# Four column tiles of one width in the joined slot's second product, and a new table of order

## The chip, the cores and the metric

The kernel runs on one core of a Trainium2 chip. The metric is the time of one execution in device microseconds; a profile of one such execution shows what each engine did. TensorE (PE in the rows, with its weight loads as PEld) multiplies, VectorE (DVE), ScalarE (ACT) and GpSimd (POOL) do the rest, SyncE (SP) issues most transfers.

## The reference

Two layers stand behind each other. The first is a gated linear recurrence over 4 sequences of 5056 rows of 256 channels; the second sends each of the 20224 rows to at most one of eight experts.

```
a_t = exp(8 * sigmoid(r_gate) * log(clip(sigmoid(a_param))))
x_gated = sqrt(max(1 - a_t * a_t, 1e-6)) * sigmoid(i_gate) * x
h = a_t[:, t] * h + x_gated[:, t]          # for each t; y[:, t] = h
...
do_compute = y @ w_skip > 0                # rows without it leave as they are
e_idx = argmax(y @ w_gate)                 # of the rows with it
h = relu(y @ w1[e]);  out = y + gate * (h @ w2[e])   # w1: 256 x 1024, w2: 1024 x 256
```

## The kernel before

The recurrence works on 40 groups of 512 rows. For each, SP loads the two gates and x, TensorE turns them so that channels lie on partitions, ScalarE and VectorE form decay and input, VectorE scans, and TensorE turns the result back. Then scores are taken (`scores`, `tally`), each row gets a place in its expert's region of a buffer in DRAM (`xs`), and GpSimd writes it there (`send`).

The experts work on slots: 256 or 128 rows of one expert, fetched from its region. A slot is turned (`turn`, L806), split into a half-precision value and its remainder (`turn_hi` on ScalarE, `turn_lo` on VectorE), multiplied by w1 (`mm1`, L827), put through relu (`relu` on ScalarE, L837) with its remainder (`rest` on VectorE, L841), multiplied by w2 (`mm2`, L853), weighed and added (`weighed`, L863), and written out (`put`, L869). Each product is a sum of three, since both factors are split. A slot of 128 rows works in two steps `q` of four 128-column pieces of the hidden layer, a slot of 256 rows in four. 48 slots stand in `STREAM` and run while the recurrence still does; behind them come the rests of the eight regions. Five of these are slots of 128 rows, three, of the experts 3, 5 and 7 (`JOINED`), share one slot of 128 rows with 32, 32 and 64 rows (`LAST`). This is the class `Joined`; its tiles end in `j`. Its `mm1` (L913) writes each expert's rows as columns of one tile. Its `mm2` (L928) has the rows as the columns of the weights that TensorE holds, so it uses a part of TensorE's columns for each expert (`tile_position`), 32, 32 and 64 wide.

In program order the last slots are s46, s52, s54, the joined slot, s48, s49 and s50. An `xrs` buffer, one of three, holds a slot's rows from its fetch until its `put` is done.

Nothing sets the order at run time. Every piece of work is a task; `Plan.order` takes the tasks in the order of the table `ORDER` and gives each of 232 tasks that could run on two engines the engine that `ENGINES` names for it. Each engine then runs its own in that order, and semaphores make it wait for what it reads. A loop for further slots stands behind the last one and runs zero times with these inputs.

Of the kernel before, what the change touches and what calls it, by code (L numbers as in the profile page):

```python
# [22 lines left out]
    "PADDAAAAAAAADAAAAAADDAAADAADAAAAAADAAAADAAAAAAAADAAAAAAAAADAAADAAAAAAAPADADAAAADAAADAADAADDAAAAAAPAA"  # L23
    "ADAAAAAAAAAAAAADAAAPPAAAAAAAAAPPAADAADAAAAAAADPPAAADAAAAAPADDADAPAPAAPAAAAAAPAAAPAAAPAPAAPPAAAPPPAAA"
    "AAAAPAPPAPPAPPPPPAAAAAAAPPAPPAAA"
# [196 lines left out]
def kernel(  # L222
# [657 lines left out]
    class Joined(Slot):  # L880
# [39 lines left out]
        def mm2(self, q):  # L920
            if q == 0:
                self.po = ring("po", [P, ST // P, D], f"po{self.name}")
            hh = self.h.pop(q)[1]
# [315 lines left out]
    for b, ks in enumerate(batches):  # L1239
# [5 lines left out]
        for k in ks:  # L1245
            _, e, rows, _ = stream[k]
            last_of[e] = se
            if k >= full_slots and e in JOINED:
# [5 lines left out]
                if len(parts) == len(JOINED):  # L1254
                    n = joined.nq
# [71 lines left out]
```

## Time and profile before

| | |
|---|---|
| three timed runs | 662.18, 664.52, 665.43 us; median 664.52 |
| the profiled execution | 662.41 us; span from first to last instruction 660.3 us |
| busy in the span | TensorE 577.6, VectorE 509.5, ScalarE 445.7, GpSimd 331.0 us |
| granted TensorE clock, mean | 0.951 |
| the joined slot's second product (L928) | 72 matmuls, 626.62 to 637.33 us |

The busy times are sums over stages with different limits, so a share of the span says little by itself. The granted clock is the share of full speed that TensorE was allowed: 1.00 is 2.4 GHz, 0.50 is 1.2 GHz. A matmul's duration in a row is its way through the array; the next one starts long before it ends, so the step from start to start is read from a row of many.

### The profile page before, as it was taken

The page shows a single profiled execution, that of the slowest core. Times are in us where ns is not written, and L with a number is a line of the kernel's source. Part 1 is how long each engine was busy: PE and PEld are TensorE (multiplying, and loading weights), DVE is VectorE, ACT ScalarE, POOL GpSimd, SP SyncE. Part 2 cuts the span into 40 slices and gives each one's busy share as a digit, 9 for nine tenths or more (in the row PEclk, how much of TensorE's full clock was granted, in tenths as well). Part 3 has the DMA queues.
Part 4 walks back from the last instruction along what each step waited for, and adds up shares of the span by engine and source line. Part 5 has one row for each costly group of instructions (what it writes and reads, how often), then busy time and mean ns, then how long its engine had stood idle before and what let it go on. Part 6 is the DMA issues. An engine that isn't in the chain of part 4 may idle for free. (4 is left out here: it accounts for less than half of the span.)

```text
span 660.3 us, 18625 instructions
## 1 busy us (share of the span) xinstructions
PE 577.6 (87%) x7204; PEld 495.3 (75%) x7204; DVE 509.5 (77%) x1149; ACT 445.7 (68%) x647; POOL 331.0 (50%) x523
## 2 busy tenths in 40 slices
PE   1544489789899999999999999998899999999996
PEld 1333378668787888888788888897798898889865
DVE  2998989879999888898898889798785566443522
ACT  7998887878998886898888886854744423222211
POOL 5456556555574565556564575646466222441201
PEclk9955579999999999999999999999999999999999
DMA  8999988896898687777586653745353312143110
GB/s 307 358 317 337 315 272 277 275 317 188 310 330 257 244 302 247 221 246 231 196 279 221 219 198 103 260 141 174 101 170 137 89 34 89 43 139 116 39 31 22
DMA packets 72408, 134.58 MB, mean 204 GB/s; under 512 B 10291, under 2 KB 42997, under 8 KB 72320
## 3 DMA queue, kind: packets, MB, share of 16 engines
q1 hardware_dynamic: 60560, 112.58, 51.7%
q0 software_dynamic: 11488, 20.82, 8.8%
q8 instruction: 57, 0.93, 0.6%
q14 instruction: 31, 0.25, 0.1%
q10 hardware_dynamic: 272, 0.00, 0.0%
HBM read 89.48 MB, written 54.44 MB: 218 GB/s over the span
## 5 line engine op out<-in xcount | busy, mean ns | idle before, releaser
L827 PE MATMUL phs<-xhs,wsb 128*128 128x128 f16 (+1 forms) x2544 | 231.0, 246 | 7.5 <-DVE hps L841 5.0
L853 PE MATMUL pos<-wsb,hps 128*128 128x256 f16 x1896 | 227.9, 273 | 2.0 <-DVE ots L863 1.0
L709 POOL DMA_INDIRECT xs<-yr,di x158 | 177.7, 1125 | 99.8 <-issue 64.2
L827 PEld LDWEIGHTS <-wsb 128*128 128x128 f16 x2544 | 195.2, 98 | 27.5 <-issue 9.9
L853 PEld LDWEIGHTS <-hps 128*128 128x128 f16 x1896 | 181.5, 98 | 25.6 <-DVE hps L841 2.1
L837 ACT ACTIVATE hps<-phs 128x512 f16<-128x512 f32 x158 | 93.3, 594 | 107.9 <-PE phs L827 92.0
L869 POOL DMA_INDIRECT out_dram<-ots,xrs x79 | 84.1, 1065 | 150.9 <-DVE ots L863 101.3
L841 DVE SCALAR_TENSOR_TENSOR hps<-phs,hps 128x512 f16<-128x512 f32 x158 | 108.1, 687 | 52.6 <-ACT hps L837 52.2
L480 DVE TENSOR_TENSOR_SCAN a<-a,a,m 128x512 f32<-128x512 f32 (+1 forms) x78 | 97.6, 1262 | 0.3
L443 ACT ACTIVATE a<-pt,cc 128x512 f32<-128x512 f32 (+1 forms) x80 | 58.5, 774 | 6.8 <-PE pt L422 6.7
L474 DVE SCALAR_TENSOR_TENSOR m<-m,pt 128x512 f32<-128x512 f32 (+1 forms) x80 | 51.6, 670 | 1.4 <-PE pt L422 1.2
L469 DVE SCALAR_TENSOR_TENSOR i<-i,x 128x1024 f32<-128x1024 f32 (+1 forms) x40 | 48.8, 1220 | 2.3 <-DMA x<-in_x_dram 2.3
L813 ACT ACTIVATE xhs<-pxs 128x256 f16<-128x256 f32 (+1 forms) x53 | 25.9, 489 | 36.3 <-PE pxs L806 29.3
L776 DVE SCALAR_TENSOR_TENSOR wsb<-w,wsb 128x512 f16<-128x512 f32 x64 | 44.0, 699 | 7.6 <-POOL wsb L772 5.7
L863 DVE SCALAR_TENSOR_TENSOR ots<-pos,xrs 128x256 f32<-128x256 f32 x79 | 36.9, 477 | 16.7 <-PE pos L853 16.1
L422 PE MATMUL pt<-ident,r 64*128 64x64 f32 x632 | 31.2, 252 | 19.3 <-ACT r L413 12.8
L502 ACT COPY yr<-py 128x512 f32<-128x512 f32 (+1 forms) x62 | 35.1, 580 | 17.9 <-DVE yr L504 6.4
L422 PEld LDWEIGHTS pt<-ident,r 64*128 64x128 f32 x632 | 26.4, 161 | 24.5 <-issue 11.5
L466 ACT ACTIVATE m<-m,quarter 128x1024 f32<-128x1024 f32 (+1 forms) x40 | 43.4, 1131 | 0.2
L816 DVE SCALAR_TENSOR_TENSOR xhs<-pxs,xhs 128x256 f16<-128x256 f32 (+1 forms) x53 | 29.3, 553 | 18.2 <-ACT xhs L813 18.0
L772 POOL TENSOR_SCALAR wsb<-w 128x512 f16<-128x512 f32 x24 | 24.1, 1006 | 38.1 <-DMA w<-in_moe_w_dram 37.5
L413 ACT ACTIVATE r<-r 128x1024 f32<-128x1024 f32 (+1 forms) x40 | 41.6, 1043 | 1.9 <-DMA r<-in_r_gate_dram 1.8
(130 smaller groups left out, 626.6 us busy)
## 6 DMA issues: line engine op xcount, KB each, us to landing
r<-in_r_gate_dram SPq DMA_DIRECT2D x39, 512.0 KB, 5.6
x<-in_x_dram SPq DMA_DIRECT2D x39, 512.0 KB, 5.9
i<-in_i_gate_dram SPq DMA_DIRECT2D x39, 512.0 KB, 5.1
out_dram<-yr SPq DMA_DIRECT2D x39, 512.0 KB, 4.8
w<-in_moe_w_dram SPq DMA_DIRECT2D x64, 256.0 KB, 4.8
xrs<-xs SPq DMA_DIRECT2D x26, 258.0 KB, 3.5
xrs<-xs SPq DMA_DIRECT2D x27, 129.0 KB, 4.0
xs<-yr,di POOLq DMA_INDIRECT x158
```

What stands on the lines that cost most here:

```text
L422: nc.tensor.transpose(to(pt[:, h]), t[r], ident[r, r], tile_position=(HP * h, 0))
L443: nc.scalar.activation(in_two(ta[g][:, k, :tiles_of(g) * P]), tp[g][:, :, k], AF.Exp, scale=c, bias=c)
L469: nc.vector.scalar_tensor_tensor(ti[g], ti[g], 1.0, tx.pop(g), op0=ALU.add, op1=ALU.mult)
L474: nc.vector.scalar_tensor_tensor(m, m, 0.5e-3, tp[g][:, :, k], op0=ALU.max, op1=ALU.mult)
L480: nc.vector.tensor_tensor_scan(a, a, tm[g][:, k, :n], prev, op0=ALU.mult, op1=ALU.add)
L709: i = nc.gpsimd.indirect_dma_start(out=xs[:, :], out_offset=bass.IndirectOffsetOnAxis(ap=vs[s]["di"][:, c:c + 1], axis=0), in_=yrow[g][:, ...
L776: nc.vector.scalar_tensor_tensor(lo, raw[e, q], SC, hi, op0=ALU.mult, op1=ALU.subtract)
L827: nc.tensor.matmul(ph[:, c, :], lhsT=self.w.w1(k, part, q * self.fp + c), rhs=self.xx[:, xx, k, :], start=(n == 0), stop=(n == 3 * KD - 1),)
L837: nc.scalar.activation(hh[:, 0], self.h[q][0], AF.Relu)
L841: nc.vector.scalar_tensor_tensor(hh[:, 1], ph, 0.0, hh[:, 0], op0=ALU.max, op1=ALU.subtract)
L853: nc.tensor.matmul(self.po[:self.np, j, :], lhsT=hh[:, h, c, j * P:j * P + self.np], rhs=self.w.w2(f, part), start=(f == 0 and j == 0 and ...
L869: i = nc.gpsimd.indirect_dma_start(out=out[:, :], out_offset=bass.IndirectOffsetOnAxis(ap=self.at[:, j, :], axis=0), in_=self.ot.pop(j)[:s ...
```

## The change

It has two parts. The first is in the `mm2` of the joined slot: each expert's rows are cut into tiles of 32, so that 64 rows become two tiles, and all four tiles have one width. Three matmuls for each factor pair become four. The second is the table: `ORDER` and `ENGINES` are other strings (of the table's 109 changed lines one is shown).

```
-0 6 9 10 16 1606 8 1600 1552 7 1612 17 1607 1601 1 2 1608 3 19 20 12 11 1516 1609 1553 13 1613 1610 1602 22 21 23 14
...
+0 6 9 10 1600 16 1606 1573 8 18 7 4 1601 1 2 1574 1607 3 1602 1575 1608 19 11 12 13 20 21 22 23 14 26 15 27 1603 17
...
-                    for o, rows, w in self.parts:
+                    for o, w in [(o + n, w) for o, rows, w in self.parts for n in range(0, rows, 32)]:
                         nc.tensor.matmul(
-                            self.po[o:o + rows, 0, :], lhsT=hh[:, h, c, o:o + rows],
+                            self.po[o:o + 32, 0, :], lhsT=hh[:, h, c, o:o + 32],
                             rhs=w.w2(f, part), start=(f == 0 and part == 0 and h == 0),
                             stop=(f == NF - 1 and h == 1), tile_position=(0, o),
                             skip_group_check=True,
```

Each engine has nearly the same tasks as before. By `ENGINES`, three squares (L453 on ScalarE, L457 on GpSimd), one piece of the weights (L770, L772) and two roundings of y (L565, L567) go from GpSimd to ScalarE, and two copies out of PSUM from VectorE to ScalarE. The filler memsets on GpSimd (L704) are 198 in place of 188. How many tasks stand ahead of a slot, counted in the two orders (before, now):

| | TensorE, ahead of `mm1` | VectorE, ahead of `turn_lo` | ScalarE, ahead of the first `relu` |
|---|---|---|---|
| slot s0 | 35, 36 | 123, 122 | 85, 88 |
| slot s12 | 138, 139 | 328, 316 | 213, 220 |
| slot s24 | 288, 290 | 588, 582 | 367, 376 |
| slot s36 | 431, 431 | 821, 818 | 499, 505 |

On TensorE, in the middle of the joined slot's second product, this stood before (`hpj` are the two tiles of the joined hidden layer, one for each half, `poj` is the result):

```order
L928 LDWEIGHTS hpj_11384
L928 MATMUL poj<-wsb,hpj_11384 32x256
L928 LDWEIGHTS hpj_11384
L928 MATMUL poj<-wsb,hpj_11384 32x256
L928 LDWEIGHTS hpj_11384
L928 MATMUL poj<-wsb,hpj_11384 64x256
L928 LDWEIGHTS hpj_11409
L928 MATMUL poj<-wsb,hpj_11409 32x256
```

That is the last group of the first half, 32, 32 and 64 columns wide, and the first load and matmul of the second half (`hpj_11409`). At the same place now:

```order
L928 LDWEIGHTS hpj_11394
L928 MATMUL poj<-wsb,hpj_11394 32x256
L928 LDWEIGHTS hpj_11394
L928 MATMUL poj<-wsb,hpj_11394 32x256
L928 LDWEIGHTS hpj_11394
L928 MATMUL poj<-wsb,hpj_11394 32x256
L928 LDWEIGHTS hpj_11394
L928 MATMUL poj<-wsb,hpj_11394 32x256
L827 LDWEIGHTS wsb
L827 MATMUL phs_0_11471<-xhs_11466,wsb 128x128
```

A group has four matmuls of 32 columns in place of two of 32 and one of 64; and behind the first half stands the first half of the first product of slot s48 (`phs_0`), where the second half of the joined product stood.

On VectorE, around the joined slot, before (`xhs` is the rounding of the slot behind it, `hps` its hidden layer, `otj` the joined result, weighed; `ots_0_11394` the result of s54):

```order
L1002 CAST tab<-ptab 1x174
L841 SCALAR_TENSOR_TENSOR hpj_11384<-phj_11238,hpj_11384 128x512
L863 SCALAR_TENSOR_TENSOR ots_0_11394<-pos_11201,xrs_10883 128x256
L841 SCALAR_TENSOR_TENSOR hpj_11409<-phj_11311,hpj_11409 128x512
L816 SCALAR_TENSOR_TENSOR xhs_11407<-pxs_11399,xhs_11407 128x256
L863 SCALAR_TENSOR_TENSOR otj_11486<-poj,xrj 128x256
L841 SCALAR_TENSOR_TENSOR hps_0_11538<-phs_0_11488,hps_0_11538 128x512
L841 SCALAR_TENSOR_TENSOR hps_1_11541<-phs_1_11513,hps_1_11541 128x512
```

There the joined result waits for nothing but its product, with the two remainders of s48 behind it. The same stretch of VectorE now:

```order
L1002 CAST tab<-ptab 1x174
L863 SCALAR_TENSOR_TENSOR ots_0_11403<-pos_11208,xrs_10930 128x256
L841 SCALAR_TENSOR_TENSOR hpj_11394<-phj_11248,hpj_11394 128x512
L816 SCALAR_TENSOR_TENSOR xhs_11466<-pxs_11414,xhs_11466 128x256
L841 SCALAR_TENSOR_TENSOR hpj_11468<-phj_11321,hpj_11468 128x512
L841 SCALAR_TENSOR_TENSOR hps_0_11496<-phs_0_11471,hps_0_11496 128x512
L863 SCALAR_TENSOR_TENSOR otj_11548<-poj,xrj 128x256
L841 SCALAR_TENSOR_TENSOR hps_1_11575<-phs_1_11550,hps_1_11575 128x512
L816 SCALAR_TENSOR_TENSOR xhs_11594<-pxs_11591,xhs_11594 128x256
```

The result of s54 is weighed ahead of the joined slot's first remainder and no longer behind it, the rounding of s48 ahead of the second, and the joined result is weighed between the two remainders of s48 and no longer ahead of both.

## Rows read from the trace of the kernel before

**Rows 1.** The page: busy us, share and instructions; TensorE's tenths in 40 slices.

```profile
PE 577.6 (87%) x7204; PEld 495.3 (75%) x7204; DVE 509.5 (77%) x1149; ACT 445.7 (68%) x647; POOL 331.0 (50%) x523
...
PE   1544489789899999999999999998899999999996
```

**Rows 2.** Stages: stretch, length, busy time of each engine, TensorE clock, DMA share, GB/s.

```profile
core 0: us, PE busy (x) PEld busy (x) DVE busy (x) ACT busy (x) POOL busy (x), PEclk, DMA share, GB/s
0.00:33.00 33.00, 10.58 (x136) 7.61 (x137) 21.39 (x40) 26.68 (x31) 15.57 (x29) 1.00 0.92 333
33.00:91.00 58.00, 29.82 (x364) 21.86 (x366) 54.01 (x114) 51.77 (x71) 35.39 (x35) 0.50 0.95 321
91.00:150.00 59.00, 50.85 (x732) 43.04 (x725) 50.86 (x117) 47.27 (x72) 32.88 (x48) 0.97 0.85 277
150.00:626.60 476.60, 459.02 (x5698) 402.69 (x5695) 375.38 (x866) 314.86 (x466) 241.89 (x404) 1.00 0.56 184
626.60:637.30 10.70, 10.70 (x74) 4.91 (x74) 1.02 (x2) 0.87 (x2) 1.16 (x3) 1.00 0.09 25
637.30:660.30 23.00, 16.57 (x221) 15.23 (x220) 6.84 (x12) 4.24 (x8) 4.14 (x6) 0.94 0.08 27
```

**Rows 3.** The end in time: start, us, engine, line, what, count [idle before, releaser].

```profile
626.62 10.71 PE L928 MATMUL poj<-wsb,hpj 128*32 128x256 f16 x72
...
637.26 2.85 PE L827 MATMUL phs<-xhs,wsb 128*128 128x128 f16 x48
637.37 0.48 DVE L863 SCALAR_TENSOR_TENSOR otj<-poj,xrj 128x256 f32<-128x256 f32 x1 [8.71 <-PE poj L928]
...
651.03 2.84 PE L853 MATMUL pos<-wsb,hps 128*128 128x256 f16 x24
...
653.91 0.48 DVE L863 SCALAR_TENSOR_TENSOR ots<-pos,xrs 128x256 f32<-128x256 f32 x1 [1.36 <-PE pos L853]
654.67 0.98 POOL L869 DMA_INDIRECT out_dram<-ots,xrs  x1 [3.04 <-DVE ots L863]
```

**Rows 4.** Line L928: duration ns min/median/max, first and last start, forms.

```profile
L928 PEld LDWEIGHTS <-hpj x72: 91/93/107, 626.6 to 637.0; 128*32 128x32 f16 x48, 128*64 128x64 f16 x24
L928 PE MATMUL poj<-wsb,hpj x72: 282/283/298, 626.6 to 637.0; 128*32 128x256 f16 x48, 128*64 128x256 f16 x24
```

**Rows 5.** TensorE in time, first 0.1 us of L928, then first 0.2.

```profile
626.62 0.29 PE L928 MATMUL poj<-wsb,hpj 128*32 128x256 f16 x2
...
626.62 0.51 PE L928 MATMUL poj<-wsb,hpj 128*32 128x256 f16 x3
```

**Rows 6.** In time, full width: a slot of 256 rows, second product.

```profile
606.20 4.09 PE L853 MATMUL pos<-wsb,hps 128*128 128x256 f16 x36
```

**Rows 7.** Scores, four tiles of 32 columns: in time from 214.4, then L533's durations.

```profile
214.47 0.59 PEld L533 LDWEIGHTS lg<-a,wr 128*32 128x32 f32 x16
214.48 1.07 PE L533 MATMUL lg<-a,wr 128*32 128x256 f32 x16
...
L533 PE MATMUL lg<-a,wr x208: 376/380/636, 27.3 to 311.3; 128*32 128x256 f32 x104
```

**Rows 8.** In time: ScalarE and VectorE on the joined second half.

```profile
627.01 0.59 ACT L837 ACTIVATE hpj<-phj 128x512 f16<-128x512 f32 x1
...
627.63 0.69 DVE L841 SCALAR_TENSOR_TENSOR hpj<-phj,hpj 128x512 f16<-128x512 f32 x1 [1.34 <-ACT hpj L837]
```

**Rows 9.** SP in time: the last fetch; the page: its size, us to landing.

```profile
641.09 0.33 SPq L792 DMA_DIRECT2D xrs<-xs  x1
...
xrs<-xs SPq DMA_DIRECT2D x27, 129.0 KB, 4.0
```

**Rows 10.** ScalarE by form: count | busy us, mean ns | idle before.

```profile
L453 ACT ACTIVATE m<-a 128x1024 f32<-128x1024 f32 x34 | 35.9, 1063 | 1.9 <-DVE a L480 1.7
...
L770 ACT ACTIVATE wsb<-w 128x512 f16<-128x512 f32 x40 | 24.9, 630 | 8.1 <-DMA w<-in_moe_w_dram 7.9
```

More of the change, by code (lines that the diff above doesn't have):

```diff
@@ L22 @@
 ENGINES = (
-    "PADDAAAAAAAADAAAAAADDAAADAADAAAAAADAAAADAAAAAAAADAAAAAAAAADAAADAAAAAAAPADADAAAADAAADAADAADDAAAAAAPAA"
-    "ADAAAAAAAAAAAAADAAAPPAAAAAAAAAPPAADAADAAAAAAADPPAAADAAAAAPADDADAPAPAAPAAAAAAPAAAPAAAPAPAAPPAAAPPPAAA"
-    "AAAAPAPPAPPAPPPPPAAAAAAAPPAPPAAA"
+    "PAAAAADAAAAAADAAAAAAAAAADAAAAAAAAAAAAAAAAAAAAAAADAAAAAAAAADAAADAAADADAPAADDAAAAAAAAAAADDAADAAAAAAPAA"
+    "ADAAADAAPAAADAAADAAAAAAAAADAADPAAAAAADADAAAAADAADDDAAAAADAAAAAAPPAAAAPAAAAAAAAAPAAPAPAPAAPPAAAAPPAAA"
+    "AAAPPPPPAPPAPPPPPAPAAAAAAPAAAAAA"
 )
 ORDER = """
[109 rows of a table removed]
[109 rows of a table added]
 """
```

216 rows, old and new, of the table ORDER are left out of this document.

## The prediction

> **What bounds the kernel now.** I read the page first, then the busy time of each engine by stage, then the end in order of time. On the page TensorE is busy 577.6 us of 660.3, VectorE 509.5, ScalarE 445.7 [rows 1]; the tenths show TensorE idle for the first sixth and at nine or more after it. The stages tell why [rows 2]. From 33 to 91 us VectorE has 54.0 us of work in 58.0 and ScalarE 51.8, while TensorE has 29.8, at a granted clock of 0.50, which is the 1.2 GHz level; it had been busy 10.6 us of the 33 before. So here the recurrence sets the pace. From 150 to 626.6 us TensorE is busy 459.0 of 476.6 us at clock 1.00: that stage is TensorE's, with 17.6 us of gaps. Then comes a stretch that belongs to one line: 10.7 us with 74 matmuls, in which VectorE has 1.0 us of work, ScalarE 0.9 and the DMA engines are at 0.09.
>
> The end in order of time shows that stretch from inside [rows 3]. The second product of the joined slot (L928) runs from 626.62 for 10.71 us. VectorE idles 8.71 us until it ends, and TensorE's next work, the first product of the slot behind it, starts at 637.26. From there three slots of 128 rows follow without a pause (16.57 us busy up to the last row of matmuls, which ends at 653.87), then 0.48 us of VectorE, the last write at 654.67 and some 5 us until the span ends. Nothing else runs beside L928, so each microsecond off it comes off the end, if the three slots behind it stay as dense.
>
> **The edit of the product.** The 72 matmuls have two widths [rows 4]: 48 of 32 columns and 24 of 64, in the order 32, 32, 64. The narrow pair runs side by side: two matmuls of 283 ns each take 0.29 us together [rows 5]. With the third the row is 0.51 us long, and the third lasts 297 ns, so it starts 0.21 us after the pair, and the next pair 0.446 us after the first (10.71 / 24). Two changes of width per triple thus cost 0.21 and 0.23 us. For comparison, a matmul of the full 128 columns with the same 256 moving columns starts every (4.09 - 0.27) / 35 = 0.109 us [rows 6]. A change of width therefore costs some 0.11 us above the streaming.
>
> The change puts four tiles of 32 columns in a row, 96 matmuls in 24 groups of four, with no change of width inside. What four tiles do is in this trace already: the scores of the recurrence (L533) are 16 passes in four groups of four tiles of 32 columns. A pass lasts 0.38 us in the median, and all 16 take 1.07 us [rows 7], so a group follows the one before after about (1.07 - 0.38) / 3 = 0.23 us; that is in fp32, with the same 256 columns; were the four not side by side, 16 passes would need four times that. All 16 weight loads are through 0.59 us after the first begins, while matmuls of earlier groups still run. So I take 0.109 us a group: 24 x 0.109 = 2.62 us. The bounds: not below 2.62, since each group must stream its 256 columns; above, 24 x 0.223 = 5.35 us (half of 0.446) if every group emptied the array as every change of width does now, and 96 x 0.109 = 10.5 us if the four ran one after another, which the pair of rows 5 excludes for two tiles. The value is the one nearest to the scores' row.
>
> The Trainium skill, "TensorE: Matmul & The Clock Gate", section "Part 3: Packing small matmuls — row/col tiling", says that a weight load overlaps running matmuls only where the two use different row groups. All four tiles here use all 128 rows; by that rule each group would show its load. The scores' loads [rows 7] also use all rows and do overlap, so the trace speaks against the rule for this case; what it would give stands below as a rival.
>
> The new order also splits the product. Before, its two halves of 5.3 us stand back to back; now the first half of the next slot's first product (24 matmuls, 2.85 / 2 = 1.43 us) stands between them. That adds two changes of width, 2 x 0.11 = 0.22 us. It is also needed: the second half reads a tile that ScalarE begins at 627.01 and VectorE finishes at 627.63 + 0.69 = 628.32 [rows 8], and the first half would now end at about 626.62 + 1.31 = 627.93. With 1.43 us of other work in between nothing waits; without it 0.4 us would be late. The product then costs 2.62 + 0.22 = 2.84 us: 10.71 - 2.84 = 7.9 us go.
>
> What is late next: the three slots' own steps. ScalarE's and VectorE's steps on a slot's tile (0.60 + 0.69 us and the gaps) were done beside L928 for the first of them; now they have 1.43 us of matmuls beside them, as those of the last slot have already. I allow 0.3 us for small waits, between 0 and 1. The fetch of the last slot waits for the joined slot's buffer: it was issued at 641.09 [rows 9], 3.8 us after L928's end, and such a fetch lands in a median of 4.0 us. In the new order TensorE has 1.43 + 1.31 + 0.22 + 1.31 + 2.85 + 1.31 = 8.4 us of other work between the product and that slot's transposes, against 7.8 us: no wait, but with little to spare; a late landing costs at most a microsecond or two, and this is in the range. Sum here: 7.9 - 0.3 = 7.6 us.
>
> **The edit of the order.** The same 2745 pieces stand in another order, and some change engine. Three squares (1.06 us each on ScalarE), one weight piece (0.63) and two roundings of y go from GpSimd to ScalarE, and two copies from VectorE to ScalarE. The last four are no larger than a weight piece, so at its time ScalarE gains at most 3 x 1.06 + 5 x 0.63 = 6.3 us [rows 10]. From 150 to 626.6 us ScalarE is idle for a third (314.9 us busy of 476.6), and the three squares stand in the program's last third; this hides them. GpSimd's ten more filler memsets hide likewise: it is busy 241.9 us of that stage. The table of counts in the section on the change shows how near the orders are: ahead of slot 0's, 12's, 24's and 36's first product TensorE has the same pieces within two, VectorE 1 to 12 fewer ahead of the slot's rounding, ScalarE 3 to 9 more ahead of its first relu. What this does to the gaps is not in any row: at best it takes half of TensorE's 59.0 - 50.9 = 8.1 us of idle time between 91 and 150 us, 4 us; at worst the moved 6.3 us are paid in full. I take zero, since the nearest row, that of the long stage, shows TensorE 96% busy and so little to win or lose.
>
> Sum against the profiled execution: it took 662.4 us, with a span of 660.3. 662.4 - 7.6 = 654.8. The median of the three timed runs is 664.5, 2.1 above that execution; the same step from it gives 656.9. I predict 656.
>
> **Rivals.** (a) Loads not hidden: each group adds the time of its load to the streaming. A load of 32 columns is a row here, 0.092 us [rows 4], so the product takes 24 x (0.109 + 0.092) + 0.22 = 5.0 us, near the 5.35 of emptied groups. The gain is 10.71 - 5.0 - 0.3 = 5.4, the time 657 to 659. It is the Trainium skill's rule quoted above that would have it so. For it: no row of this trace has four fp16 tiles. Against it: rows 7. 0.11.
>
> (b) The moved work of ScalarE is paid in full: in the startup, where it is busy 51.8 of 58 us, each of its microseconds in front of the first slots' steps delays TensorE. The time is 664.5 - 7.6 + 6.3 = 663.2, no change. For it: rows 2. Against it: the squares that move stand late, where ScalarE has room. 0.17.
>
> (c) The order itself is better: VectorE has less in front of the first slots, and half of TensorE's idle time between 91 and 150 us goes. 656.9 - 4 = 653. 0.16.
>
> (d) Slower: TensorE's clock. It is granted 0.50 from 33 to 91 us and 1.00 behind that [rows 2]; a startup in another order may see it rise later. In the stage behind, TensorE is busy 50.9 us of 59, so a microsecond more at half speed costs up to 0.86 us of doubled work, less the 0.14 us of idle time that can take it up: about 0.7 us. From 11 us later on the gain of the product is gone; at 20 us later it costs 14 us and the time is 664.5 - 7.6 + 14 = 671. For it: the clock stands at the lower level once more, in the mean of 0.97 there. Against it: in both orders the same transfers and products stand in front. 0.06.
>
> **How the numbers follow.** My forecast has 0.50, and with (a) 0.11, (c) 0.16 and the small rest of (b) that ends below 661.2 the chance of faster by over 0.5% is 0.78. Less than 0.5% (3.3 us) is about what a measurement of this kernel can't tell from no change: 0.16, nearly all of it (b). Slower 0.06 is (d). The range reaches from 651 (c, with 2 us for the runs' spread) to 661.5, which takes in (a), the bound of 5.35 us and half of (b).
>
> **What would show it.** In the new profile L928 should show 96 matmuls of one form, in two rows of about 1.5 us with L827 between them, and VectorE's wait for it should fall from 8.71 us to under 3. From the start of L928 to the end of the span there should be about 26 us in place of 33.7. If L928's rows are 2.5 us or longer each, it is (a). If L928 is short and the span did not follow, the first start of L928 tells: it stands at 626.6 now, and (b), (c) and (d) move it. I am wrong if it starts more than 4 us off, or if the slots behind show waits that add up to more than 1 us.

## The result, and the profile after

The changed kernel takes 643.14 us, the median of four runs, where the kernel before takes 664.97: 21.8 us less between the medians. The ratio is 0.9688, 95% interval 0.9645 to 0.9731; by it, 20.7 us went. The forecast was 656, with 651 as the low end of its range. The direction was right and more than half of the gain was missing from the sum. The execution that was profiled took 642.77 us, with a span of 640.9; that of before 662.41, with 660.3. So the two traces differ by 19.4 us of span.

A line of the page of after, for [rows 1]: busy time of the engines.

```profile
PE 566.7 (88%) x7228; PEld 494.0 (77%) x7228; DVE 501.4 (78%) x1147; ACT 450.8 (70%) x655; POOL 332.4 (52%) x527
```

The stages of after, for [rows 2], with the same columns; the last two stretches are the product and what is behind it.

```profile
0.00:33.00 33.00, 11.80 (x154) 9.00 (x156) 20.82 (x44) 28.15 (x32) 15.29 (x29) 1.00 0.92 333
33.00:91.00 58.00, 30.71 (x386) 22.42 (x383) 52.72 (x111) 53.32 (x76) 37.56 (x35) 0.74 0.99 334
91.00:150.00 59.00, 52.47 (x764) 45.84 (x762) 52.76 (x132) 50.03 (x78) 32.91 (x52) 0.97 0.82 272
150.00:614.90 464.90, 452.20 (x5624) 399.22 (x5620) 367.02 (x850) 314.10 (x463) 242.50 (x405) 1.00 0.57 188
614.90:619.30 4.40, 4.40 (x123) 3.80 (x123) 1.81 (x3) 1.47 (x3) 0.00 (x0) 1.00 0.13 34
619.30:640.90 21.60, 15.17 (x196) 13.75 (x195) 6.24 (x11) 3.75 (x7) 4.13 (x6) 0.95 0.09 29
```

The end of after in time, for [rows 3] (start, us, engine, line, what, count, idle before and what ended it), and the forms of the product, for [rows 4].

```profile
614.91 1.49 PE L928 MATMUL poj<-wsb,hpj 128*32 128x256 f16 x48
616.34 1.51 PE L827 MATMUL phs<-xhs,wsb 128*128 128x128 f16 x24
617.78 1.49 PE L928 MATMUL poj<-wsb,hpj 128*32 128x256 f16 x48
619.33 0.48 DVE L863 SCALAR_TENSOR_TENSOR otj<-poj,xrj 128x256 f32<-128x256 f32 x1
...
634.51 0.48 DVE L863 SCALAR_TENSOR_TENSOR ots<-pos,xrs 128x256 f32<-128x256 f32 x1 [1.36 <-PE pos L853]
...
L928 PEld LDWEIGHTS <-hpj x96: 92/97/97, 614.9 to 618.9; 128*32 128x32 f16 x96
L928 PE MATMUL poj<-wsb,hpj x96: 272/273/283, 614.9 to 619.0; 128*32 128x256 f16 x96
```

Read it in two parts, cut at the start of L928. Behind the cut all is as predicted: each half of the product takes 1.43 us (614.91 to 616.34, 617.78 to 619.21), 2.86 in all; VectorE's wait for it is gone; from the start of L928 to the end of the span there are 640.9 - 614.9 = 26.0 us. Ahead of the cut 11.7 us are missing that no term of the sum held: L928 starts at 614.91, and it started at 626.62.

TensorE issues the same 6912 matmuls ahead of L928 in both kernels. Up to the cut it is busy 550.3 us of 626.6 before and 547.2 of 614.9 after, so 8.6 of the 11.7 us are idle time that went, and 3.1 are busy time. Most of the idle time did not go where I had looked: ahead of 91 us it falls by 2.1 us (from 50.6 to 48.5), and between 91 and 150 us it is 59.0 - 52.5 = 6.5 us, where it was 8.1. In the stage behind it falls from 17.6 to 12.7 us, and one stretch loses as much as that, between two points, the starts of the first product of slot s32 (its second quarter) and of slot s39. The first line is before, the second after, by stretch:

```profile
440.10:520.10 80.00, 74.24 (x874) 65.14 (x872) 57.50 (x127) 43.70 (x69) 44.66 (x70) 1.00 0.44 143
```

```profile
434.70:508.60 73.90, 73.40 (x875) 65.89 (x872) 55.41 (x133) 43.31 (x67) 43.77 (x73) 1.00 0.49 158
```

The same 875 matmuls stand with 5.8 us of gaps before and 0.5 after. I call this stretch the late one. Below, "idle in the late stretch" is always this difference, length less TensorE's busy time, between the same two matmuls of a run's own trace.

### The profile page after: what moved, and what is told of

Read it like the earlier page. It is cut to its first block, busy times and chain, and to the rows that moved or that the text cites. A ratio compares the mean times of both kernels' runs of the same rounds, so it can differ in the third digit from the quotient of the medians.

```text
span 640.9 us, 18655 instructions
## 1 busy us (share of the span) xinstructions
PE 566.7 (88%) x7228; PEld 494.0 (77%) x7228; DVE 501.4 (78%) x1147; ACT 450.8 (70%) x655; POOL 332.4 (52%) x527
## 5 line engine op out<-in xcount | busy, mean ns | idle before, releaser
L709 POOL DMA_INDIRECT xs<-yr,di x158 | 186.5, 1180 | 99.2 <-issue 56.8
L827 PE MATMUL phs<-xhs,wsb 128*128 128x128 f16 (+1 forms) x2544 | 231.5, 247 | 3.2 <-DVE hps L841 1.4
L827 PEld LDWEIGHTS <-wsb 128*128 128x128 f16 x2544 | 196.3, 99 | 21.9 <-issue 3.6
L837 ACT ACTIVATE hps<-phs 128x512 f16<-128x512 f32 x158 | 93.7, 596 | 107.2 <-PE phs L827 89.0
L869 POOL DMA_INDIRECT out_dram<-ots,xrs x79 | 86.6, 1097 | 153.3 <-DVE ots L863 87.3
L841 DVE SCALAR_TENSOR_TENSOR hps<-phs,hps 128x512 f16<-128x512 f32 x158 | 107.8, 685 | 56.6 <-ACT hps L837 55.9
L466 ACT ACTIVATE m<-m,quarter 128x1024 f32<-128x1024 f32 (+1 forms) x40 | 43.4, 1131 | 0.2
L413 ACT ACTIVATE i<-i 128x1024 f32<-128x1024 f32 (+1 forms) x40 | 41.8, 1044 | 1.4 <-DMA i<-in_i_gate_dram 1.3
L453 ACT ACTIVATE m<-a 128x1024 f32<-128x1024 f32 (+1 forms) x38 | 39.4, 1046 | 2.4 <-DVE a L480 1.4
```

The costliest lines, as they stand in the source:

```text
L413: nc.scalar.activation(t, t, AF.Tanh, scale=0.5)
L709: i = nc.gpsimd.indirect_dma_start(out=xs[:, :], out_offset=bass.IndirectOffsetOnAxis(ap=vs[s]["di"][:, c:c + 1], axis=0), in_=yrow[g][:, ...
L827: nc.tensor.matmul(ph[:, c, :], lhsT=self.w.w1(k, part, q * self.fp + c), rhs=self.xx[:, xx, k, :], start=(n == 0), stop=(n == 3 * KD - 1),)
L837: nc.scalar.activation(hh[:, 0], self.h[q][0], AF.Relu)
L841: nc.vector.scalar_tensor_tensor(hh[:, 1], ph, 0.0, hh[:, 0], op0=ALU.max, op1=ALU.subtract)
L869: i = nc.gpsimd.indirect_dma_start(out=out[:, :], out_offset=bass.IndirectOffsetOnAxis(ap=self.at[:, j, :], axis=0), in_=self.ot.pop(j)[:s ...
```

## The experiments

Each ratio is to runs of before on the same chip. The runs with the three letters alone, with all letters, with the widths and with the filler were made on a chip on which all takes longer (681.8 us for before). A part "of after's table" means order and engine letters together. The two tables hold the same tasks up to a cut but for one, at 888 and at 1606, so that one can be continued with the other there.

**Product and table apart.** First the new product in the old table:

```
-                    for o, rows, w in self.parts:
+                    for o, w in [(o + n, w) for o, rows, w in self.parts for n in range(0, rows, 32)]:
-                            self.po[o:o + rows, 0, :], lhsT=hh[:, h, c, o:o + rows],
+                            self.po[o:o + 32, 0, :], lhsT=hh[:, h, c, o:o + 32],
```

> The tables of before with the new product alone. Theory (product and order add, as the two traces read: L928 start to span end 33.7 against 26.0 us): 7.7 us under before, ratio 0.988, 657 us where before is 665. Rival (the product needs the new order around it, since its second half would wait for hpj in the old one): at most 4 us under before, ratio 0.994.

655.86 us, ratio 0.9868 (0.9819 to 0.9918), 8.8 us by it: the theory. Here the halves stand back to back, and L928 is one row of 3.03 us with 96 matmuls. The second half's input is late, as predicted, but by no more than that: its first weight load waits 0.33 us for VectorE's L841, where the prediction had 0.4.

Then the new table with the old product:

```
-ENGINES, ORDER = before's
+ENGINES, ORDER = after's
```

> The tables of after with the old product of 72 matmuls in tiles of 32, 32 and 64 columns. Theory: the order alone is worth what L928's start shows, 11.7 us in the profiled executions, to 14 us (the rest of the 21.8 us between the medians): ratio 0.979 to 0.983, 651 to 653 us where before is 665; L928 itself is back at some 10.7 us. Rival (the order gains only because of the four-column product, or the 11.7 us are one execution's chance): ratio over 0.993.

654.24 us, ratio 0.9824 (0.9784 to 0.9863), 11.7 us. The product of the two ratios is 0.9694, and after has 0.9688: the parts add. I had valued the second at zero.

**Where the table gains.** Its halves, cut at task 1606 (slot s23):

```
+ORDER = after[:1606] + [t for t in before if t not in after[:1606]]
```

> Old product. The table of after for its first 1606 tasks (up to slot s23's second product, 336 us), then the remaining tasks in before's order with before's engines; the two tables hold the same tasks up to there but for one. Theory (each stretch is worth what the two traces show for it by itself): L853 of s23 comes 6.4 us earlier and the end with it, ratio 0.990. Rival A (the whole gain is TensorE's clock in the startup, 61.4 against 34.1 us at half speed): ratio 0.980 as the whole table. Rival B (a gain made early is lost again in the late stretch, whose other engines wait for something else): within 0.4% of before.

660.01 us, ratio 0.9918 (0.9877 to 0.9958).

```
+ORDER = before[:1606] + [t for t in after if t not in before[:1606]]
```

> Old product. The table of before for its first 1606 tasks, then the remaining tasks in after's order with after's engines. Theory (stretches add): the waits of TensorE between 440 and 520 us go (5.8 against 0.5 us idle), 5.3 us under before, ratio 0.992. Rival A (all of the gain is made in the startup): within 0.3% of before, with the waits at 440 to 520 us still there. Rival B (the late stretch is the whole gain, the early one only moves it): ratio 0.982.

659.0 us, ratio 0.9907 (0.9876 to 0.9937), and the late stretch shows 0.25 us of idle time:

```profile
440.40:514.00 73.60, 73.35 (x874) 65.89 (x872) 55.48 (x133) 43.28 (x67) 43.86 (x73) 1.00 0.48 159
```

The halves give 0.9826 together, the whole table 0.9824. Both rivals of each fall: neither half is the whole, and no gain is lost later.

The early half was cut once more, to its first 397 tasks (94 us):

```
+ORDER = after[:397] + [t for t in before if t not in after[:397]]
```

> Before, old product; the first 397 tasks (up to slot s1's first product, 94 us) in after's order with after's engines, the rest in before's. Theory (each stretch for itself): TensorE's idle time ahead of s0's first product falls by 2 us (50.4 against 48.3 us in the two first traces), and 2 of the 5.4 us of the early half are there: ratio 0.997. Rival A (the startup is all of the early half): 0.992. Rival B (a gain in the startup is used up by slot s14, since VectorE, 87 us busy of the next 97, is behind anyway): 1.000 with idle at s14 as before's 65.0 us.

661.64 us, ratio 0.9946 (0.9916 to 0.9976), idle ahead of s0's first product 48.4 us: the gain of the startup is clear of zero, but its size is not settled. The interval reaches from 1.6 to 5.6 us and holds both the theory (2 us, 0.997) and rival A (the whole early half, 0.992).

Then to the tasks 888 to 1606:

```
+ORDER = before[:888] + [t for t in after[:1606] if t not in before[:888]] + [the rest, as in before]
```

> Before, old product; only the tasks 888 to 1606 (slot s11's first product to s23's second, 191 to 336 us) in after's order with after's engines. Theory: 3 of the early half's 5.4 us are here, ratio 0.995, idle between s11 and s23 down from 5.8 to under 3 us. Rival (these waits are only the late end of what the startup left behind, VectorE's queue of work): ratio 1.000 and idle 5 us or more.

665.4 us, ratio 0.9976 (0.994 to 1.0011): idle from s11 to s23 4.8 us in place of 5.8, and no change of time that can be told from none; the interval also holds the theory's 0.995. The tasks between 397 and 888 were not tried by themselves.

Two of VectorE's waits in the startup differ plainly. Up to s0's first product, before and then the run with after's first 397 tasks (waited for, us, times, longest):

```profile
DVE wsb L776 <- POOL wsb L772: 5.7, 3, 2.8
```

```profile
DVE i L469 <- ACT i L413: 3.9, 2, 3.3
...
DVE wsb L776 <- ACT wsb L770: 1.7, 2, 1.5
...
DVE wsb L776 <- POOL wsb L772: 1.5, 3, 0.5
```

VectorE waits 2.5 us less for the first parts of weights, but 3.9 us for a gate from ScalarE, a wait that before's list does not have; its idle time up to there is 16.8 us (86.9 less 70.1 busy) and was 15.4 (87.5 less 72.1). So the shorter wait for weights does not explain the startup's gain, and its cause stays open.

**What the late stretch lost.** In before's trace, in time:

```profile
452.59 3.75 POOL L457 TENSOR_TENSOR m<-a 128x1024 f32<-128x1024 f32 x2
452.81 3.63 DVE L619 TENSOR_TENSOR d<-ls 128x64 f32<-128x64 f32 x1
...
456.60 0.68 DVE L841 SCALAR_TENSOR_TENSOR hps<-phs,hps 128x512 f16<-128x512 f32 x1
457.34 0.93 PE L827 MATMUL phs<-xhs,wsb 128*128 128x256 f16 x7 [2.38 <-DVE hps L841]
```

```profile
L619 DVE TENSOR_TENSOR d<-ls x7: 208/216/3628, 339.8 to 554.2; 128x64 f32<-128x64 f32 x6, 128x48 f32<-128x48 f32 x1
```

L619 adds 64 numbers a row, and its seven runs take 0.216 us in the median (the last line: ns, least, median, most). Here it takes 3.63 and ends 0.1 us after GpSimd's two squares of 1024. L841 stands behind it in VectorE's queue, though ScalarE had its input ready at 452.97, and TensorE waits for that. The Trainium skill, "SBUF — State Buffer", section "Who interferes with whom", says that a VectorE instruction with two SBUF inputs contends with a GpSimd instruction that reads SBUF, and that the second to start is blocked until the first is through. The trace agrees that it is held, with 3.63 against 0.216 us; but L619 starts 0.2 us behind the first square and is held through the second as well, which the sentence does not cover. It is no chance of one execution: in the seven traces with the three squares on GpSimd, one instruction of VectorE lasts 3.4 to 4.2 us beside the two that stand together, and in the nine without them none is held for longer than 1.3 us.

The new table puts the squares of groups 36, 37 and 38 on ScalarE. These three letters alone, in the old table with the old product:

```
-    "ADAAAAAAAAAAAAADAAAPPAAAAAAAAAPPAADAADAAAAAAADPPAAADAAAAAPADDADAPAPAAPAAAAAAPAAAPAAAPAPAAPPAAAPPPAAA"
+    "ADAAAAAAAAAAAAADAAAPPAAAAAAAAAPPAADAADAAAAAAADAAAAADAAAAAAADDADAPAPAAPAAAAAAPAAAPAAAPAPAAPPAAAPPPAAA"
```

> Before, with the squares (L457) of the groups 36, 37 and 38 on ScalarE in place of GpSimd: three letters of the string of engines, no other task moved. In before's trace VectorE's L619 of 0.22 us takes 3.63 us at 452.8 beside two of them, and TensorE waits for VectorE's L841 behind it. Theory (this collision is the late stretch's loss): L619 back at 0.22 us, TensorE's idle time between the starts of s32's and s39's first products 5.8 us down to under 1.5 us, ratio 0.992 as for the late half of the table. Rival A (the collision explains the one wait of 2.4 us and the order the rest): idle 3 to 4 us, ratio 0.996. Rival B (ScalarE, with three more tasks, is late instead): ratio 1.000 or over, TensorE waiting for ScalarE there.

Ratio 0.9895 (0.9859 to 0.993), and no instruction of VectorE is held there any more. With before's table on this chip it is another one than L619 (from the widths' run below, whose late stretch is before's), a step of one element a row with a median of 0.15 us:

```profile
466.77 3.80 DVE L951 SCALAR_TENSOR_TENSOR sel<-nxt,base 128x1 f32<-128x1 f32 x1
```

The idle time did not fall to the 1.5 us that the theory had: the late stretch keeps 5.3 us, where the widths' run has 8.7. Part of it is a wait of 2.5 us behind a block of ScalarE's work, which is read below in the run that adds the product. The ratio says 7 us, the trace 3.4.

All 54 letters in the old order:

```
-ENGINES = before's
+ENGINES = after's
```

> Before's order with all 54 changed engine letters of after, old product. Theory: the late stretch's gain is in the letters (5 us) and the early one's in the order, so ratio 0.992, idle at s23 within 1 us of before's 68.4 us. Rival A (letters are all of it): 0.982. Rival B (letters picked for another order collide anew in this one): ratio over 0.998, with new long instructions on VectorE beside GpSimd's.

Ratio 1.0686 (1.0618 to 1.0754): 47 us slower. The sign is rival B's, but neither its size nor its mechanism was expected: no instruction of VectorE is stretched anew. VectorE waits for GpSimd's parts of the weights instead, 25.1 us in six waits, the longest 12.5, where the widths' run has 5.7 us in three:

```profile
DVE wsb L776 <- POOL wsb L772: 25.1, 6, 12.5
```

In the longest of them GpSimd waits for no other engine: it works through eight sends (L709, some 0.98 us each) from 117.7 to 130.2 us, and the weight part, which stands behind them in its queue, starts at 130.27. So the 54 letters as a whole fit only the order they were chosen with. Where the rest of the 47 us goes was not followed.

The reverse, after with the three squares back on GpSimd:

```
-    "ADAAADAAPAAADAAADAAAAAAAAADAADPAAAAAADADAAAAADAADDDAAAADAAAAAAPPAAAAPAAAAAAAAAPAAPAPAPAAPPAAAAPPAAA"
+    "ADAAADAAPAAADAAADAAAAAAAAADAADPAAAAAADADAAAAADPPDDDAAAADPAAAAAPPAAAAPAAAAAAAAAPAAPAPAPAAPPAAAAPPAAA"
```

> After with the squares of groups 36, 37 and 38 back on GpSimd, three letters. Theory (the collision with VectorE is in the letters and not in before's order): a VectorE instruction of two inputs from SBUF is held up by some 2 to 3.5 us beside L457, and TensorE's late stretch (s32 to s39) idles 2 to 4 us more than after's 0.5 us: ratio to before 0.973 to 0.976. Rival (the new order has slack there or puts no such instruction beside them): 0.969 as after.

652.67 us, ratio 0.98 (0.9752 to 0.9848), somewhat more than expected, and 5.8 us of idle time are back in the late stretch. Another instruction of VectorE is held up beside the squares, L658. It reads one tile, and its row begins 0.36 us ahead of the first square's, so it has neither two inputs nor is it the second to start. In time, with a stretch in the columns of [rows 2] as the last line:

```profile
454.59 4.15 DVE L658 TENSOR_SCALAR sg<-sg 128x8 f32<-128x8 f32 x1
...
454.95 3.75 POOL L457 TENSOR_TENSOR m<-a 128x1024 f32<-128x1024 f32 x2
455.90 1.48 PE L827 MATMUL phs<-xhs,wsb 128*128 128x256 f16 x12
458.74 2.19 ACT L466 ACTIVATE m<-m,quarter 128x1024 f32<-128x1024 f32 x2 [4.34 <-POOL m L457]
461.31 1.06 ACT L502 COPY yr<-py 128x512 f32<-128x512 f32 x2
461.96 0.69 DVE L504 COPY yr<-py 128x512 f32<-128x512 f32 x1 [3.10 <-POOL still L704]
462.71 0.58 PE L422 MATMUL pt<-ident,i 64*128 64x64 f32 x6 [4.01 <-DVE yr L504]
464.97 2.74 PE L827 MATMUL phs<-xhs,wsb 128*128 128x256 f16 x12
...
462.70:469.00 6.30, 6.20 (x53) 4.82 (x54) 4.86 (x12) 1.40 (x3) 3.12 (x5) 0.53 0.07 22
```

But TensorE's wait of 4.01 us does not come from it. VectorE is free again at 458.74 and then idles 3.10 us ahead of L504. By the trace's semaphores L504 waits for ScalarE (the row names a filler of GpSimd that ended last before it), whose copy L502 stands behind the roots L466, and the roots waited 4.34 us for the squares themselves. So the squares on GpSimd cost here by the roots that read them, and this run does not show that VectorE's held instruction costs anything. The wait also has a price behind it: in the 6.3 us that follow, the granted clock is 0.53 (the 1.2 GHz level), and twelve matmuls of L827 take 2.74 us where twelve took 1.48 at 1.00. The late stretch is 82.1 us long in place of after's 73.9, 5.3 us of it more idle time and 2.9 us more busy time for the same matmuls.

Next the three letters and the new product together in the old order:

```
-ORDER, ENGINES, product = before's
+ORDER = before's, ENGINES = before's with the three letters, product = after's
```

> Before's order with the three squares on ScalarE and the product in four tiles of 32 columns: the two edits measured alone gave 0.9868 and 0.9895. Theory (they add, being far apart in time): 0.976. Rival (the tail's end is set by the last rows written, so that the second gain is partly lost): 0.982 or over.

654.0 us, ratio 0.9834 (0.9783 to 0.9885): a miss. Beside the product alone (0.9868) the letters are worth 2 us here, though by the two intervals that could be anything from none to the 7 us above. The trace shows what is left. The collision is gone, but the squares now stand on ScalarE in one block with a table load and the roots, ahead of a L837 that TensorE needs:

```profile
461.38 2.02 ACT L453 ACTIVATE m<-a 128x1024 f32<-128x1024 f32 x2
...
463.43 1.28 ACT L466 ACT_TABLE_LOAD   x1
...
464.72 2.19 ACT L466 ACTIVATE m<-m,quarter 128x1024 f32<-128x1024 f32 x2
466.82 1.06 ACT L837 ACTIVATE hps<-phs 128x512 f16<-128x512 f32 x2
467.42 0.69 DVE L841 SCALAR_TENSOR_TENSOR hps<-phs,hps 128x512 f16<-128x512 f32 x1 [5.31 <-ACT hps L837]
...
468.17 1.47 PE L827 MATMUL phs<-xhs,wsb 128*128 128x256 f16 x12 [2.53 <-DVE hps L841]
```

After's order has the squares far apart and the roots earlier. So three tasks were moved to where ScalarE idled in this trace (1325 and 1315 are the squares, 1328 the roots, the other numbers are their neighbours in the table):

```
-2308 2318 2305 ... 2343 1280 ... 1290 1265 ... 2329 1264 1325 1315 1328 2323
+2308 2318 1325 2305 ... 2343 1315 1280 ... 1290 1328 1265 ... 2329 1264 2323
```

> As the run before it (before's order, three squares on ScalarE, product in four tiles), with three tasks of ScalarE moved: the squares of groups 37 and 36 stand behind slot s33's and s34's L813 where ScalarE idled 1.6 and 0.9 us, and the roots L466 behind the exponential L651 at 456, where it idled 2.9 us; they had stood in one block of 5.5 us ahead of a L837 for which VectorE and then TensorE waited. Theory (the late stretch's loss is the collision plus this block): TensorE's idle time between s32's and s39's first products 3.8 us down to under 1.5 us, ratio 0.977 to 0.980. Rival (the wait goes to the next task of ScalarE, so that only the whole new order helps): idle 3 us or more, ratio 0.983 as before it.

648.21 us, ratio 0.9752 (0.9713 to 0.9791). The three tasks fit into ScalarE's pauses, and the late stretch has 0.5 us of idle time:

```profile
449.59 1.05 ACT L453 ACTIVATE m<-a 128x1024 f32<-128x1024 f32 x1
450.62 0.60 ACT L813 ACTIVATE xhs<-pxs 128x512 f16<-128x512 f32 x1
451.11 1.05 ACT L453 ACTIVATE m<-a 128x1024 f32<-128x1024 f32 x1
...
456.20 1.28 ACT L466 ACT_TABLE_LOAD   x1
457.50 2.19 ACT L466 ACTIVATE m<-m,quarter 128x1024 f32<-128x1024 f32 x2
```

```profile
439.50:513.50 74.00, 73.48 (x874) 65.37 (x873) 52.74 (x127) 45.83 (x72) 38.77 (x69) 1.00 0.47 153
```

And the same with after's first 397 tasks in front:

```
+ORDER = after[:397] + [t for t in the table above if t not in after[:397]]
```

> The run beside it with the first 397 tasks in after's order and letters as well: startup, three letters, three moved tasks and the product, all else as before. Theory (the parts add, and with 1.6 us of the middle left out they are nearly all of the change): startup 0.9946 times 0.978, so 0.972 to 0.975, where after stands at 0.9688. Rival (the startup's gain is lost in what follows): 0.978 or over.

646.42 us, ratio 0.9713 (0.967 to 0.9756), beside 0.9688 for the whole change: product, startup, three letters and three places are nearly all of it. Its interval overlaps with that of the run before it (0.9752), so what the startup adds there is not shown by itself.

**The price of a width.** Old tiles of 32, 32 and 64 columns in the old table, the loops turned so that the width changes once a half:

```
+            for width in (32, 64):
                 for c in range(self.fp):
...
-                    for o, rows, w in self.parts:
+                        for o, rows, w in [x for x in self.parts if x[1] == width]:
```

> Before's tables and tiles (32, 32 and 64 columns), but in each half first the 24 matmuls of 32 columns and then the 12 of 64, so that the width changes once where it changed 24 times. Theory (a change of width costs, not the third tile): 24 steps of 0.109 us and one or two changes, 2.7 to 3.0 us a half, L928 5.4 to 6.0 us in place of 10.71. Rival A (72 matmuls of three tiles cost what they cost): 10 us or more. Rival B (matmuls of one tile behind one another wait for each other's sums): the 12 of 64 columns at some 0.22 us each, 4 us a half, 8 us in all.

One execution, of 679.04 us: the product runs from 648.30 to the start of the next one at 653.99, 5.69 us, where by [rows 3] it ran from 626.62 to 637.26, 10.64 us.

```profile
L929 PE MATMUL poj<-wsb,hpj x72: 272/273/297, 648.3 to 653.8; 128*32 128x256 f16 x48, 128*64 128x256 f16 x24
...
653.99 2.85 PE L827 MATMUL phs<-xhs,wsb 128*128 128x128 f16 x48
```

With 48 steps (24 pairs, 24 of 64 columns) at 0.109 us, 5.2 of the 5.69 us are streaming. The width changes 3 times in place of 47, and 4.95 us for 44 changes are 0.11 us each, as read from [rows 5]. The other 2.6 us come from four tiles side by side (24 steps in place of 48).

**The clock of the startup.** Matmuls that nothing reads, to keep TensorE busy, in after:

```
+            if t.engine == "PE" and at < 377:
+                for _ in range(12):
+                    nc.tensor.matmul(filler[:, 0, :P], lhsT=ones, rhs=ones, start=True, stop=True)
```

> After, with 12 matmuls of 128 columns that nothing reads, behind each of TensorE's 36 tasks ahead of slot s0's first product (432 in all). It asks whether the granted clock of 0.5 in the startup costs time. Theory A (the clock is a result of TensorE's waiting there and costs little, since VectorE and the transfers end last): clock 0.9 or more from 33 to 91 us, time within 0.5% of after, ratio to before 0.966 to 0.972. Theory B (half clock stretches the chain): slot s0's first product 2 to 5 us earlier than after's 85.9 us, ratio under 0.964. Rival (the filler delays the transposes more than the clock gives): ratio over 0.975.

Ratio 0.9942 (0.9908 to 0.9975), so some 17 us slower than after at 0.9688: the rival.

```profile
33.00:91.00 58.00, 42.34 (x576) 32.65 (x574) 44.52 (x98) 46.21 (x63) 28.45 (x30) 0.82 0.83 275
```

From 33 to 91 us TensorE is busy 42.3, VectorE gets only 44.5 us of work done, and s0's first product comes at 108.5 us, on a chip where the old table has it at 92. By the order of the program the filler stands in TensorE's queue ahead of transposes that VectorE needs; that this is the whole loss was not tried. The question itself was answered by two other runs of the same chip, whose tables are the same up to there. The run with three letters (first) and that of the widths:

```profile
33.00:92.00 59.00, 26.51 (x332) 19.25 (x333) 50.98 (x107) 48.59 (x65) 37.77 (x35) 0.53 0.95 312
```

```profile
33.00:92.00 59.00, 26.93 (x333) 19.55 (x333) 50.39 (x106) 49.04 (x66) 37.17 (x35) 1.00 0.94 317
```

One was granted 0.53 (close to the 1.2 GHz level) and the other 1.00 (2.4 GHz), TensorE's busy time is the same within 0.5 us, and s0's first product starts at 92.62 and 92.19 us. Six traces of other chips with before's startup agree: from 33 to 87 us three were granted 0.50 to 0.56, and s0's first product starts at 87.5 us in each; three were granted 0.89 to 1.00, and it starts no earlier, at 88.5 to 88.9.

## Why the prediction was right and wrong

- **The product: right.** 2.84 us predicted, 2.86 measured. 0.109 us a group from [rows 6], no extra time between groups of one width, and 0.11 us for a change all held. Rival (a) falls: the 96 loads of 92 to 97 ns, on all 128 rows, lie inside 2.86 us. The rule of the Trainium skill that would have shown them ("TensorE: Matmul & The Clock Gate", "Part 3: Packing small matmuls — row/col tiling") does not hold for this case.
- **Behind the product: right.** 26.0 us to the end, as said; the fetch of the last slot was in time, and the last step of VectorE has the same 1.36 us of wait as in [rows 3].
- **The order: the step that failed.** "What this does to the gaps is not in any row ... I take zero, since the nearest row, that of the long stage, shows TensorE 96% busy and so little to win or lose." The runs showed 11.7 us (ratio 0.9824), 6 of it in the late half and 5 in the early. L928 starts 11.7 us earlier, and the prediction had named more than 4 us as the sign of being wrong. A share of 96% over 476.6 us leaves 17.6 us, twice the gain of the product, and before's trace showed a part of them: L619 with a maximum of 3.63 us beside a median of 0.216. I had read the end by instruction and the long stage by its mean only.
- **The three squares: the sign was wrong.** I priced them as work that ScalarE takes on, 1.06 us each, hidden or (rival b) paid in full. What they did on GpSimd decided: there they held VectorE for 3.4 us, and TensorE waited 2.38 us behind it. Back on GpSimd in the new order they cost some 7 us (0.98 against 0.9688), by another way: ScalarE's roots waited for them, and TensorE's clock fell behind the wait.
- **Rival (c)** had the direction, with 4 us and the wrong place: between 91 and 150 us only 1.6 us went. Its bound, half of one stage's idle time, was no bound of the table's effect.
- **Rival (d)** took a price of 0.86 us, 0.7 less the idle time, for each microsecond at the lower clock in the dense stage. That is twice too much: a microsecond at half the clock still does half its work. The run with the squares back on GpSimd has 2.9 us more busy time for 6.3 us at a clock of 0.53, some 0.46 us each. In the startup, where TensorE waits for others, the price was nothing that shows. And its condition did not come: from 33 to 91 us the granted clock is 0.74 in the mean after, where it was 0.50.

What stays open: 3.1 of the 11.7 us between the two traces are TensorE's busy time ahead of L928, which differs between executions (553.7 us in the run with the new table alone, 547.2 in after), and I can't tie it to the change; the granted clock is no reason, for behind s0's first product its mean is 0.99 in both traces. The letters alone gave 7 us by the ratio on one chip and 2 on another, with 3.4 and 1.9 us in the late stretch; the intervals are too wide to call these different. The early half is shown as a gain (0.9918), and in it the startup's (0.9946); which wait makes it, and what the tasks between 397 and 888 add, is not shown.

## What to carry to other kernels

Before a change of order is given zero, add up the gaps inside the dense stage and look, form by form, for an instruction whose longest run is many times its median: each may be a wait that another table loses. An instruction that changes engine is priced on both: what it costs where it goes, and what waited for it, or was held beside it, where it was. Letters of engine and order belong together: the same 54 letters were part of an 11.7 us gain in their own order, and cost 47 us in the other.

## What the runs showed of the hardware

- A VectorE instruction of 64 elements a row lasted 3.63 us beside two squares of GpSimd (3.75 us together); one of 8 elements, L658, 4.15 us; one of a single element, L951, 3.80 us. All three ended within 0.1 us of the second square, not of the first.
- Two tiles of 32 columns beside one of 64 cost 0.446 us a triple when the widths alternate, and about two steps of 0.109 us when each width stands by itself (5.69 us for 24 triples with three changes): the change of width is the difference.
- At a granted clock of 0.53 or 1.00, 333 matmuls of the startup took TensorE 26.5 and 26.9 us, and the next stage began within 0.5 us of the same time.
- Behind a wait of 4.01 us in the dense stage TensorE's granted clock was 0.53 for 6.3 us, and twelve matmuls took 2.74 us in place of 1.48.
